# Re-ordering three stretches of a TensorE-bound attention and feed-forward kernel: other PSUM banks for block 0's last columns, batch 1's keys by values inside an output tile, batch 2's numerators later and in two pairs of banks

## Chip, cores, metric

One core of one Trainium2 chip. The metric is the device time of one execution in microseconds; medians of several executions are quoted. The span of a profile runs from its first to its last instruction and is some 1.85 us shorter than the time of the same execution.

## The reference

```python
q_p, k_p = phi(q), phi(k)              # relu, times cos and sin of the position, side by side: 128 features
kv  = einsum('bhsf,bhsd->bhfd', k_p, v)    # "keys by values", per batch and head
num = einsum('bhsf,bhfd->bhsd', q_p, kv)   # "numerators"
den = einsum('bhsf,bhf->bhs', q_p, k_p.sum(2)) + 1e-6
x   = (num / den) reshaped to 4608 tokens x 512
out = (gelu(x @ w_gate) * (x @ w_val)) @ w_out
```

8 batches of 576 tokens, 8 heads of 64; the feed-forward part has width 1536. Inputs are float32, the matmuls run in bf16.

## The kernel before

Everything is hand-scheduled: instructions run on each engine in the order in which the program names them. `ps` is the whole PSUM, eight banks of 512 float32 columns. The feed-forward part works in blocks of tokens (block 0 is batch 0's 576 tokens, then blocks of 512, the last of 448); attention of the next batch is slipped between the matmuls of a block.

```python
def kv_half(b, g, bank, eng="s"):        # keys by values of 4 heads: 20 matmuls into ps[:, bank], then a copy
    ...
def numer(b, t, bank, rows=128):         # numerators of token tile t: 8 matmuls into bank and bank + 1
    numer_mm(b, t, bank, 0, rows)
    numer_mm(b, t, bank, 1, rows)
    xb = new_xb()
    norm(xb, bank, 0, 2, rows)           # VectorE: den + eps, 1 / den, numerators * (1 / den)
    return xb
def gate(n, jt, c0, w, gb): ...          # 4 matmuls into bank gb, then ScalarE's gelu out of it
def value(n, jt, c0, w, vb): ...         # 4 matmuls into bank vb, then VectorE's multiply hT = gel * value
def o_part(n, m, bank, j0, j1): ...      # matmuls j0..j1 of the 12 of an output tile of 128 tokens
def x_by_pe(b, t, xb, bank, eng): ...    # 4 transposes on TensorE into a bank, then a copy into xT
def turn_x(b, t, xb): ...                # the same by DMA transpose from SyncE's queue
...
# block 0's last columns (A = columns 0-255, Bw = 256-575; X(t) transposes tile t, Y(t) its numerators)
gv_unit(0, 0, 256, 128, 5, 6)
X(3, 0, "s")()
gv_unit(0, 1, 256, 128, 4, 7)
Y(4, 0)()
gv_unit(0, 0, 384, 128, 5, 2)
...
# between block 0 and block 1
o_tile(0, 1, 5)
kv_half(1, 0, 6, "s")
kv_half(1, 1, 7, "v")
...
# block 1: what is put between gate and value of a unit (mid) or after it
def attn_step(b, i):
    if i == 0:
        kv_half(b, 0, 6)
        kv_half(b, 1, 7)
    else:
        turn_x(b, i - 1, numer(b, i - 1, 6))
...
mid[1][0].append(L(attn_step, 1, 5))     # batch 1's last tile
...
put(5 + s, L(attn_step, b, 0))           # batch b = 2: after unit 4, as s = -1 for block 1
for i in range(5):
    mid[n][6 + s + i].append(L(attn_step, b, i + 1))
```

Of the kernel before, what the change touches and what calls it, by code (L numbers as in the profile page):

```python
# [16 lines left out]
def kernel(  # L17
# [133 lines left out]
    def kv_half(b, g, bank, eng="s"):  # L151
        for h in range(4 * g, 4 * g + 4):
            for j in range(NJ + 1):
                nc.tensor.matmul(  # L154
                    ps[:, bank, (h % 4) * (D + 1):(h % 4 + 1) * (D + 1)],
                    lhsT=kp[:, j, h, :],
                    rhs=vx[b % 2][:, j, h, 0:D + 1],
                    start=(j == 0), stop=(j == NJ),
                )
        if eng is not None:  # L160
            kv_evac(b, g, bank, eng)

    def kv_evac(b, g, bank, eng):
        src = ps[:, bank, 0:4 * (D + 1)].rearrange("p (h e) -> p h e", e=D + 1)
        dst = kv[b % 2][:, 4 * g:4 * g + 4, 0:D + 1]
        (nc.scalar.copy if eng == "s" else nc.vector.tensor_copy)(dst, src)

    def numer_mm(b, t, bank, g, rows=128):
        for h in range(4 * g, 4 * g + 4):
            nc.tensor.matmul(  # L170
                ps[0:rows, bank + g, (h % 4) * (D + 1):(h % 4 + 1) * (D + 1)],
                lhsT=qT[b % 2][:, t, h, 0:rows],
                rhs=kv[b % 2][:, h, 0:D + 1],
                start=True, stop=True,
            )

    def norm(xb, bank, g0, g1, rows=128):

        n = g1 - g0
        nd = ps[0:rows, bank + g0:bank + g1, 0:4 * (D + 1)].rearrange("p g (h e) -> p g h e", e=D + 1)  # L180
        den = rot.tile([128, 2, 4], FP32, name="den")
        nc.vector.tensor_scalar(den[0:rows, 0:n], nd[:, :, :, D], EPS, None, op0=ALU.add)  # L182
        rec = rot.tile([128, 2, 4], FP32, name="rec")
        nc.vector.reciprocal(rec[0:rows, 0:n], den[0:rows, 0:n])
        nc.vector.tensor_tensor(  # L185
            xb[0:rows, g0:g1], nd[:, :, :, 0:D],
            rec[0:rows, 0:n, :, None].to_broadcast([rows, n, 4, D]), op=ALU.mult,
        )

    def new_xb():  # L190
        return rot.tile([128, 2, 4, D], BF16, name="xb", bufs=4)

    def numer(b, t, bank, rows=128):
# [4 lines that stand above are left out]
        norm(xb, bank, 0, 2, rows)  # L198
        return xb

    def turn_x(b, t, xb):
        p0 = b * S + t * 128
        xb2 = xb.rearrange("p g h d -> p (g h d)")
        if t < NJ:
            nc.sync.dma_start_transpose(out=xT[:, :, p0:p0 + 128], in_=xb2)
        else:
            xr = rot.tile([128, CT, 128], BF16, name="xr")
            nc.sync.dma_start_transpose(out=xr, in_=xb2)
            nc.gpsimd.tensor_copy(xT[:, :, p0:p0 + 64], xr[:, :, 0:128:2])  # L209
# [15 lines left out]
    def value(n, jt, c0, w, vb):  # L225

        p0 = starts[n] + c0
        for ct in range(CT):
            nc.tensor.matmul(  # L229
                ps[:, vb, 0:w], lhsT=wv_sb[:, ct, jt * 128:(jt + 1) * 128],  # L230
                rhs=xT[:, ct, p0:p0 + w], start=(ct == 0), stop=(ct == CT - 1),
            )
        gel = gels.pop((n, jt, c0))
        nc.vector.tensor_mul(hT[n % 2][:, jt, 64 + c0:64 + c0 + w], gel[:, 0:w], ps[:, vb, 0:w])  # L234

    def gv_unit(n, jt, c0, w, gb, vb, mid=()):
        gate(n, jt, c0, w, gb)
        for f in mid:
            f()
        value(n, jt, c0, w, vb)  # L240
# [15 lines left out]
    def o_part(n, m, bank, j0, j1):  # L256
        c0 = 128 * m - starts[n] + 64
        for jt in range(j0, j1):
            nc.tensor.matmul(  # L259
                ps[:, bank, :], lhsT=hT[n % 2][:, jt, c0:c0 + 128], rhs=wo_sb[:, jt, :],  # L260
                start=(jt == 0), stop=(jt == JT - 1),
            )
        if j1 == JT:
            o_store(m, bank)

    def o_tile(n, m, bank):

        o_part(n, m, bank, 0, JT)
# [45 lines left out]
    def load_v(b):  # L314
        load(vf, v, b)
# [20 lines left out]
    def x_by_pe(b, t, xb, bank, eng, c0=0, c1=CT):  # L336
        p0 = b * S + t * 128
        cp = nc.vector.tensor_copy if eng == "v" else nc.scalar.copy
        xb2 = xb.rearrange("p g h d -> p (g h d)")
        rows = 128 if t < NJ else 64  # L340
        view = ps[:, bank, 0:256].bitcast(BF16).rearrange("p (c t) -> p c t", c=CT)
        for ct in range(c0, c1):
            nc.tensor.transpose(  # L343
                out=view[:, ct, 0:rows], in_=xb2[0:rows, ct * 128:(ct + 1) * 128], identity=ident[0:rows, 0:rows],
            )
        cp(xT[:, c0:c1, p0:p0 + rows], view[:, c0:c1, 0:rows])  # L346

    def sq(j, which, eng, *h):
        scale(Q, j, which, eng, *h)
# [48 lines left out]
    A, Bw = (0, 256), (256, 320)  # L398
    xs = {1: x1}

    def X(t, bank, eng):
        return lambda: x_by_pe(0, t, xs[t], bank, eng)

    def Y(t, bank):
        def f():
            xs[t] = numer(0, t, bank, 128 if t < NJ else 64)
        return f
# [20 lines left out]
    value(0, 3, *A, 2)  # L428
    q_by_pe(0, 4, 3, "s")
    gv_unit(0, 0, 256, 128, 5, 6)  # L430
    X(3, 0, "s")()
    gv_unit(0, 1, 256, 128, 4, 7)
    Y(4, 0)()
    gv_unit(0, 0, 384, 128, 5, 2)
    gv_unit(0, 1, 384, 128, 4, 3)
    gate(0, 4, *A, 5)
    X(4, 0, "v")()
    gate(0, 5, *A, 4)
    gv_unit(0, 2, *Bw, 1, 6)
    gv_unit(0, 3, *Bw, 0, 7)  # L440
    value(0, 4, *A, 3)
    value(0, 5, *A, 2)
    gv_unit(0, 0, 512, 64, 4, 6)
    gv_unit(0, 1, 512, 64, 5, 7)
# [10 lines left out]
    def L(f, *a):  # L455
        return lambda: f(*a)
# [15 lines left out]
    for jt in range(4, 12):  # L472
        for i, (c0, w) in enumerate((A, Bw)):
            if (jt, i) not in ((4, 0), (5, 0)):
                gv_unit(0, jt, c0, w, i, 3 - i)
            for f in between.get((jt, i), ()):
                f()
    for j in range(NJ + 1):
# [7 lines left out]
    cast_v(1, 4, 6, "v")  # L486
    cast_v(1, 6, 8, "s")
    load_v(2)
    o_tile(0, 1, 5)
    kv_half(1, 0, 6, "s")  # L490
    kv_half(1, 1, 7, "v")
    y = [new_xb() for _ in range(4)]
    o_part(0, 2, 4, 0, 4)
    for g in (0, 1):
        numer_mm(1, 0, 0, g)
        numer_mm(1, 1, 2, g)
    norm(y[0], 0, 0, 2)
    norm(y[1], 2, 0, 2)
    o_part(0, 2, 4, 4, 8)
    for g in (0, 1):  # L500
        numer_mm(1, 2, 6, g)
    norm(y[2], 6, 0, 2)
    x_by_pe(1, 0, y[0], 0, "s")
    o_part(0, 2, 4, 8, 12)
    x_by_pe(1, 1, y[1], 1, "s")
    for g in (0, 1):
        numer_mm(1, 3, 2, g)
    norm(y[3], 2, 0, 2)
    o_part(0, 3, 5, 0, 5)
    x_by_pe(1, 2, y[2], 6, "s")  # L510
    o_part(0, 3, 5, 5, 10)
    x_by_pe(1, 3, y[3], 7, "s")
    for j in range(NJ + 1):
        sq(j, 0, "v")
    o_part(0, 3, 5, 10, 12)
    sq(0, 1, "s")

    def attn_step(b, i):

        if i == 0:  # L520
            kv_half(b, 0, 6)
            kv_half(b, 1, 7)
        else:
            turn_x(b, i - 1, numer(b, i - 1, 6))


    after = {n: {jt: [] for jt in range(JT)} for n in range(NB)}

    mid = {n: {jt: [] for jt in range(JT)} for n in range(NB)}
    mid[1][0].append(L(attn_step, 1, 5))  # L530
    for n in range(1, 7):
        b = n + 1
        a = after[n]

        def put(u, *fs):
            a[u].extend(fs)

        s = 0 if n > 1 else -1
        if n > 1:
            put(0, L(sq, 0, 0, "v"), L(sq, 1, 0, "v"), L(sq, 1, 1, "v"), L(sq, 0, 1, "s"))  # L540
            put(1, L(sq, 2, 0, "v"), L(sq, 2, 1, "s"), L(turn_q, b, 0, 3))
            put(1, L(sq, 3, 0, "v"), L(sq, 4, 0, "v"), L(sq, 4, 1, "v"), L(sq, 3, 1, "s"), L(turn_q, b, 3, 5))
        else:
            put(0, L(sq, 1, 1, "s"), L(sq, 2, 1, "v"), L(turn_q, b, 0, 3))
            put(0, L(sq, 3, 1, "v"), L(sq, 4, 1, "s"), L(turn_q, b, 3, 5))
        put(2 + s, L(sk, 0, 0, "v"), L(sk, 1, 0, "v"), L(sk, 0, 1, "s"), L(sk, 1, 1, "s"))
        put(3 + s, L(sk, 2, 0, "v"), L(sk, 3, 0, "v"), L(sk, 4, 0, "v"))
        put(3 + s, L(sk, 2, 1, "s"), L(sk, 3, 1, "s"), L(sk, 4, 1, "s"), L(cast_v, b, 0, 4))
        put(4 + s, L(cast_v, b, 4, 8, "s"))
        put(5 + s, L(attn_step, b, 0))  # L550
        if b + 1 < B:

            for f, u in zip((load_q, load_k, load_v), (3, 4, 5) if n > 1 else (1, 10, 11)):
                put(u, L(f, b + 1))
        for i in range(5):
            mid[n][6 + s + i].append(L(attn_step, b, i + 1))

    for n in range(2, NB):
        for i, m in enumerate(o_tiles_of(n - 1)):
# [47 lines left out]
```

## Time and profile before

| | before |
|---|---|
| median of the first three executions | 326.73 us (326.55 to 326.76) |
| the execution that was profiled | 327.47 us, span 325.6 us |
| TensorE busy | 318.2 us, 98% |
| VectorE, ScalarE, GpSimd busy | 52%, 46%, 7% |
| TensorE's late rows, worked out in the prediction | 1.94 us in seven places, all between 22 and 71 us |

SyncE's queue, from the timeline of the kernel before (start, time until the issue is done, queue, line, operation):

```profile
61.85 1.21 SPq L208 DMA_TRANSPOSE xr<-xb  x1
63.23 7.74 SPq L145 DMA_TRANSPOSE qT<-qp  x2
```

Batch 2's queries (`qT<-qp`) stand behind batch 1's last tile (`xr<-xb`), which stands behind the loads of batch 2. The first of the two landed at 70.73.

### The profile page before, as it was taken

To read this page: it belongs to the slowest core of one execution; us is meant where nothing else is said; L and a number is where in the kernel's file an instruction comes from. 1 tells how busy PE (TensorE), PEld (TensorE's weight loads), DVE (VectorE), ACT (ScalarE), POOL (GpSimd) and SP (SyncE) were. 2 spreads that over 40 slices of the span, in tenths; PEclk is the share of its full clock that TensorE was granted. 3 is DMA by queue.
4 is the path that set the end of the run, shared out by engine and by line. 5 is a ranking of instruction groups with operands and counts; after the bars stand their busy time and mean duration, and the time that the engine had idled before them with its cause. 6 is when DMAs were issued, how large, how long until landed. Compare 5 with 4: busy or idle time off the path is not lost.

```text
span 325.6 us, 5865 instructions
## 1 busy us (share of the span) xinstructions
PE 318.2 (98%) x2218; PEld 167.1 (51%) x2218; DVE 168.7 (52%) x380; ACT 151.3 (46%) x271; POOL 21.8 (7%) x43
## 2 busy tenths in 40 slices
PE   7999999999999999999999999999999999999994
PEld 2587866455445444554455445544554444444443
DVE  4885776768653666365736474537454222222210
ACT  5674664863483256425652475237622322323321
POOL 2651010000100010001000100010000100100000
PEclk9999999999999999999999999999999999999999
DMA  7999999999899939992899379975434111000024
GB/s 221 287 204 275 232 286 294 338 169 207 268 229 322 249 50 172 317 255 64 162 329 253 64 133 280 308 92 106 121 64 83 32 32 34 32 32 32 35 65 97
DMA packets 88300, 55.56 MB, mean 171 GB/s; under 512 B 53072, under 2 KB 83536, under 8 KB 88272
## 3 DMA queue, kind: packets, MB, share of 16 engines
q1 hardware_dynamic: 81744, 48.84, 61.7%
q0 software_dynamic: 6096, 5.90, 10.2%
q10 hardware_dynamic: 432, 0.46, 0.5%
q8 instruction: 17, 0.28, 0.4%
q14 instruction: 11, 0.09, 0.1%
HBM read 37.75 MB, written 9.44 MB: 145 GB/s over the span
## 4 chain that ended last, share of the span: by engine, by line
PE 94%; DMA 2%; DVE 1%; issue 1%; ACT 1%; ACTq 0%
PE ps L218 28%; PE ps L259 28%; PE ps L229 28%; PE ps L170 3%; PE ps L127 3%; PE ps L154 2%; DMA qT<-qp 2%; PE ps L324 1%; PE ps L277 1%; PE ps L343 1%; DVE vx L141 0%; ACT xT L346 0%; DVE qT L332 0%; DVE qp L135 0%; DVE xb L185 0%
## 5 line engine op out<-in xcount | busy, mean ns | idle before, releaser
L234 DVE TENSOR_TENSOR hT<-gel,ps 128x512 bf16<-128x512 f32 (+5 forms) x126 | 76.0, 608 | 88.8 <-PE ps L229 86.7
L218 PE MATMUL ps<-xT,wg_sb 128*128 128x512 bf16 (+5 forms) x504 | 113.4, 349 | 0.2 <-ACT xT L346 0.2
L229 PE MATMUL ps<-xT,wv_sb 128*128 128x512 bf16 (+5 forms) x504 | 113.2, 348 | 0.0
L223 ACT ACTIVATE gel<-ps 128x512 f32<-128x512 f32 (+5 forms) x126 | 67.4, 536 | 75.1 <-PE ps L218 46.6
L259 PE MATMUL ps<-wo_sb,hT 128*128 128x512 bf16 x420 | 96.5, 379 | 0.0
L218 PEld LDWEIGHTS <-wg_sb 128*128 128x128 bf16 x504 | 47.1, 98 | 45.3 <-issue 0.7
L229 PEld LDWEIGHTS <-wv_sb 128*128 128x128 bf16 x504 | 45.6, 98 | 38.9 <-issue 0.2
L259 PEld LDWEIGHTS <-hT 128*128 128x128 bf16 x420 | 40.8, 98 | 47.7
L288 ACT COPY o_sb<-ps 128x512 f32<-128x512 f32 x35 | 20.5, 586 | 75.2 <-PE ps L259 72.1
L182 DVE TENSOR_SCALAR den<-ps 128x8 f32<-128x8 f32 (+2 forms) x41 | 6.7, 165 | 44.4 <-PE ps L170 44.4
L185 DVE TENSOR_TENSOR xb<-ps,rec 128x512 bf16<-128x512 f32 (+2 forms) x41 | 27.8, 678 | 1.5
L137 ACT ACTIVATE kp<-kf,sin_c 128x512 bf16<-128x512 f32 (+1 forms) x41 | 25.4, 679 | 0.8 <-DMA kf<-in_k_dram 0.8
L170 PEld LDWEIGHTS <-qT 128*128 128x128 bf16 (+1 forms) x320 | 15.1, 98 | 9.1 <-DMA qT<-qp 0.8
L135 DVE TENSOR_SCALAR kp<-kf,cos_c 128x512 bf16<-128x512 f32 (+1 forms) x45 | 18.7, 463 | 1.4 <-DMA kf<-in_k_dram 1.4
L137 ACT ACTIVATE qp<-qf,sin_c 128x512 bf16<-128x512 f32 x28 | 19.3, 713 | 0.0
L135 DVE TENSOR_SCALAR qp<-qf,cos_c 128x512 bf16<-128x512 f32 x40 | 18.0, 492 | 0.1
L170 PE MATMUL ps<-kv,qT 128*128 128x65 bf16 (+1 forms) x320 | 16.5, 194 | 0.7 <-DMA qT<-qp 0.4
L209 POOL COPY xT<-xr 128x256 bf16<-128x256 bf16 x7 | 2.8, 401 | 198.6 <-DMA xr<-xb 198.6
L127 PE MATMUL ps<-hT 128*128 128x512 bf16 x34 | 11.0, 478 | 1.7 <-DVE par_i L104 1.7
L154 PEld LDWEIGHTS <-kp 128*128 128x128 bf16 x320 | 10.9, 97 | 2.6 <-issue 0.7
L154 PE MATMUL ps<-vx,kp 128*128 128x65 bf16 x320 | 11.1, 193 | 0.1
L141 ACT CAST vx<-vf 128x1280 bf16<-128x1280 f32 (+1 forms) x9 | 9.7, 1074 | 1.1 <-DMA vf<-in_v_dram 1.1
(54 smaller groups left out, 88.9 us busy)
## 6 DMA issues: line engine op xcount, KB each, us to landing
out_dram<-o_sb SPq DMA_DIRECT2D x38, 128.0 KB, 2.4
kf<-in_k_dram SPq DMA_DIRECT2D x7, 640.0 KB, 8.2
out_dram<-o_sb SPq DMA_DIRECT2D x16, 256.0 KB, 2.9
qf<-in_q_dram SPq DMA_DIRECT2D x6, 640.0 KB, 6.1
vf<-in_v_dram SPq DMA_DIRECT2D x6, 640.0 KB, 9.6
kf<-in_k_dram SPq DMA_DIRECT2D x7, 512.0 KB, 6.5
qf<-in_q_dram SPq DMA_DIRECT2D x6, 512.0 KB, 4.8
vf<-in_v_dram SPq DMA_DIRECT2D x6, 512.0 KB, 8.6
```

The lines of the kernel that those rows point to most:

```text
L127: nc.tensor.matmul(ps[:, bank, :], lhsT=junk[:, 0:128], rhs=junk, start=True, stop=True)
L135: nc.vector.tensor_scalar(d, s, col, 0.0, op0=ALU.mult, op1=ALU.max)
L137: nc.scalar.activation(d, s, AF.Relu, scale=col)
L154: nc.tensor.matmul(ps[:, bank, (h % 4) * (D + 1):(h % 4 + 1) * (D + 1)], lhsT=kp[:, j, h, :], rhs=vx[b % 2][:, j, h, 0:D + 1], start=(j == ...
L170: nc.tensor.matmul(ps[0:rows, bank + g, (h % 4) * (D + 1):(h % 4 + 1) * (D + 1)], lhsT=qT[b % 2][:, t, h, 0:rows], rhs=kv[b % 2][:, h, 0:D ...
L185: nc.vector.tensor_tensor(xb[0:rows, g0:g1], nd[:, :, :, 0:D], rec[0:rows, 0:n, :, None].to_broadcast([rows, n, 4, D]), op=ALU.mult,)
L218: nc.tensor.matmul(ps[:, gb, 0:w], lhsT=wg_sb[:, ct, jt * 128:(jt + 1) * 128], rhs=xT[:, ct, p0:p0 + w], start=(ct == 0), stop=(ct == CT - 1),
L223: nc.scalar.activation(gel[:, 0:w], ps[:, gb, 0:w], AF.Gelu)
L229: nc.tensor.matmul(ps[:, vb, 0:w], lhsT=wv_sb[:, ct, jt * 128:(jt + 1) * 128], rhs=xT[:, ct, p0:p0 + w], start=(ct == 0), stop=(ct == CT - 1),
L234: nc.vector.tensor_mul(hT[n % 2][:, jt, 64 + c0:64 + c0 + w], gel[:, 0:w], ps[:, vb, 0:w])
L259: nc.tensor.matmul(ps[:, bank, :], lhsT=hT[n % 2][:, jt, c0:c0 + 128], rhs=wo_sb[:, jt, :], start=(jt == 0), stop=(jt == JT - 1),)
L288: nc.scalar.copy(o_sb, ps[:, bank, :])
```

## The change

Its intent: let no engine make TensorE wait between 22 and 71 us. Three parts: other banks and another order for block 0's last columns; keys by values six matmuls earlier, with the second output tile split around them, so that more matmuls are left to cover the copies just before block 1; batch 2's first numerators behind unit 5 of block 1 and batch 1's last ones in unit 3; batch 2's five groups take banks 6/7 and 4/5 in turn.

```diff
@@ -428,17 +428,16 @@
     value(0, 3, *A, 2)
     q_by_pe(0, 4, 3, "s")
     gv_unit(0, 0, 256, 128, 5, 6)
-    X(3, 0, "s")()
-    gv_unit(0, 1, 256, 128, 4, 7)
-    Y(4, 0)()
-    gv_unit(0, 0, 384, 128, 5, 2)
-    gv_unit(0, 1, 384, 128, 4, 3)
+    gv_unit(0, 1, 256, 128, 4, 7, (X(3, 0, "s"),))
+    Y(4, 2)()
+    gv_unit(0, 0, 384, 128, 5, 1)
+    gv_unit(0, 1, 384, 128, 4, 0)
     gate(0, 4, *A, 5)
-    X(4, 0, "v")()
+    X(4, 7, "v")()
     gate(0, 5, *A, 4)
-    gv_unit(0, 2, *Bw, 1, 6)
-    gv_unit(0, 3, *Bw, 0, 7)
-    value(0, 4, *A, 3)
+    gv_unit(0, 2, *Bw, 2, 6)
+    gv_unit(0, 3, *Bw, 3, 7)
+    value(0, 4, *A, 1)
     value(0, 5, *A, 2)
     gv_unit(0, 0, 512, 64, 4, 6)
     gv_unit(0, 1, 512, 64, 5, 7)
@@ -472,7 +471,8 @@
     for jt in range(4, 12):
         for i, (c0, w) in enumerate((A, Bw)):
             if (jt, i) not in ((4, 0), (5, 0)):
-                gv_unit(0, jt, c0, w, i, 3 - i)
+                j = 0 if jt == 4 else i
+                gv_unit(0, jt, c0, w, j, 3 - j)
             for f in between.get((jt, i), ()):
                 f()
     for j in range(NJ + 1):
@@ -486,48 +486,49 @@
     cast_v(1, 4, 6, "v")
     cast_v(1, 6, 8, "s")
     load_v(2)
-    o_tile(0, 1, 5)
+    o_part(0, 1, 5, 0, 6)
     kv_half(1, 0, 6, "s")
     kv_half(1, 1, 7, "v")
+    o_part(0, 1, 5, 6, 12)
     y = [new_xb() for _ in range(4)]
-    o_part(0, 2, 4, 0, 4)
     for g in (0, 1):
         numer_mm(1, 0, 0, g)
         numer_mm(1, 1, 2, g)
     norm(y[0], 0, 0, 2)
     norm(y[1], 2, 0, 2)
-    o_part(0, 2, 4, 4, 8)
+    o_part(0, 2, 4, 0, 6)
     for g in (0, 1):
         numer_mm(1, 2, 6, g)
     norm(y[2], 6, 0, 2)
     x_by_pe(1, 0, y[0], 0, "s")
-    o_part(0, 2, 4, 8, 12)
+    o_part(0, 2, 4, 6, 10)
     x_by_pe(1, 1, y[1], 1, "s")
     for g in (0, 1):
         numer_mm(1, 3, 2, g)
     norm(y[3], 2, 0, 2)
-    o_part(0, 3, 5, 0, 5)
+    o_part(0, 2, 4, 10, 12)
+    o_part(0, 3, 5, 0, 2)
     x_by_pe(1, 2, y[2], 6, "s")
-    o_part(0, 3, 5, 5, 10)
+    o_part(0, 3, 5, 2, 7)
     x_by_pe(1, 3, y[3], 7, "s")
+    o_part(0, 3, 5, 7, 12)
     for j in range(NJ + 1):
         sq(j, 0, "v")
-    o_part(0, 3, 5, 10, 12)
     sq(0, 1, "s")
 
-    def attn_step(b, i):
+    def attn_step(b, i, bank=6):
 
         if i == 0:
             kv_half(b, 0, 6)
             kv_half(b, 1, 7)
         else:
-            turn_x(b, i - 1, numer(b, i - 1, 6))
+            turn_x(b, i - 1, numer(b, i - 1, bank))
 
 
     after = {n: {jt: [] for jt in range(JT)} for n in range(NB)}
 
     mid = {n: {jt: [] for jt in range(JT)} for n in range(NB)}
-    mid[1][0].append(L(attn_step, 1, 5))
+    mid[1][3].append(L(attn_step, 1, 5))
     for n in range(1, 7):
         b = n + 1
         a = after[n]
@@ -553,7 +554,9 @@
             for f, u in zip((load_q, load_k, load_v), (3, 4, 5) if n > 1 else (1, 10, 11)):
                 put(u, L(f, b + 1))
         for i in range(5):
-            mid[n][6 + s + i].append(L(attn_step, b, i + 1))
+
+            where = mid[n][6 + s + i] if n > 1 or i else after[n][5]
+            where.append(L(attn_step, b, i + 1, 6 if n > 1 or i % 2 == 0 else 4))
 
     for n in range(2, NB):
         for i, m in enumerate(o_tiles_of(n - 1)):
```

## The prediction

> **What bounds the kernel now.** I read the page first (busy shares, then the chain that ended last), then the list of waits, then TensorE's rows in order of time.
>
> ```profile
> PE 318.2 (98%) x2218; PEld 167.1 (51%) x2218; DVE 168.7 (52%) x380; ACT 151.3 (46%) x271; POOL 21.8 (7%) x43
> ...
> PE 94%; DMA 2%; DVE 1%; issue 1%; ACT 1%; ACTq 0%
> ```
>
> TensorE is the bound: 98% busy, 94% of the chain, nobody else above 52%. The change removes no instruction, so it can win only the time in which TensorE stands still. The list of waits shows very little of that:
>
> ```profile
> PE ps L170 <- DMA qT<-qp: 0.4, 1, 0.4
> PE ps L218 <- ACT xT L346: 0.2, 1, 0.2
> PE ps L170 <- ACT xT L346: 0.2, 1, 0.2
> ```
>
> These are three waits of 0.8 us in all (the fourth, 1.7 us, is the start of the kernel). The rows in time show more, if one subtracts starts from starts. Columns: start, length, engine, line, operation, form, count, and in brackets the idle time that the profile admits:
>
> ```profile
> 22.72 0.39 PE L229 MATMUL ps<-xT,wv_sb 128*128 128x128 bf16 x4
> 23.15 0.40 PE L343 MATMUL ps<-ident,xb 128*128 128x128 bf16 x4
> 23.38 0.39 PE L218 MATMUL ps<-xT,wg_sb 128*128 128x128 bf16 x4
> 23.61 0.39 PE L229 MATMUL ps<-xT,wv_sb 128*128 128x128 bf16 x4
> 24.22 0.41 PE L170 MATMUL ps<-kv,qT 128*64 128x65 bf16 x8 [0.23 <-ACT xT L346]
> ...
> 30.73 0.71 PE L229 MATMUL ps<-xT,wv_sb 128*128 128x320 bf16 x4
> 31.42 0.70 PE L218 MATMUL ps<-xT,wg_sb 128*128 128x320 bf16 x4
> 32.08 0.70 PE L229 MATMUL ps<-xT,wv_sb 128*128 128x320 bf16 x4
> ...
> 53.89 0.42 PE L170 MATMUL ps<-kv,qT 128*128 128x65 bf16 x8
> 54.29 0.40 PE L343 MATMUL ps<-ident,xb 128*128 128x128 bf16 x4
> ...
> 58.47 0.59 PE L259 MATMUL ps<-wo_sb,hT 128*128 128x512 bf16 x2
> 59.30 1.02 PE L218 MATMUL ps<-xT,wg_sb 128*128 128x512 bf16 x4 [0.24 <-ACT xT L346]
> ...
> 69.39 1.03 PE L218 MATMUL ps<-xT,wg_sb 128*128 128x512 bf16 x4
> 70.78 0.43 PE L170 MATMUL ps<-kv,qT 128*128 128x65 bf16 x8 [0.35 <-DMA qT<-qp]
> ```
>
> The undisturbed step from start to start is 0.216 us at 512 columns (24 of them between 45.27 and 50.45), 0.136 at 320, 0.056 at 128, and 0.032 for the 65-column ones. So the 23.15 row was due at 22.72 + 4 x 0.056 = 22.94 and is 0.21 late. Likewise: 24.22 is 0.39 late, 31.42 is 0.15, 32.08 is 0.12, 54.29 is 0.14, 59.30 is 0.40, 70.78 is 0.53. Together **1.94 us**. After 71 us I find no late row: TensorE runs without a break to the end, so all that can be won lies in these seven places, and whatever is won there reaches the end unchanged.
>
> **What the Trainium skill says.** "Perfetto Trace Analysis", section "Tensor Engine Instruction (MATMUL, LD_WEIGHTS)": the profiler computes a matmul's end from its size, it doesn't observe it. The trace agrees: a row of four 512-column matmuls is 1.03 long while the next starts after 0.865, so every wait is shown some 0.16 too short, and shorter ones not at all. "TensorE: Matmul & The Clock Gate", "Back-to-back issue gap": N/2.4 + 2.5 ns, 216 ns at 512 columns; the trace has 0.216. "PSUM — Partial Sum Buffer", "PSUM bank collisions raise a hardware error": guard a bank as a whole by semaphores, not by address. That is why a writer waits for the last reader of its bank; the 24.22 row waits for ScalarE's copy out of the bank it reuses. The same page, "Engine vs sequencer instructions": ScalarE and VectorE queues are strict FIFO, which decides the second loss below.
>
> **The change part by part.**
>
> *Block 0's last columns.* (a) The transposes of tile 3 move behind the next gate group (0.22 us of matmuls), past the end of VectorE's multiply at 23.09, which they waited for: -0.21. (b) Tile 4's numerators get banks 2 and 3 instead of the bank that tile 3's copy is leaving: their wait (0.39) goes. But the gate group behind them reads the columns that this copy writes. Transposes at 23.17, end of their output 0.40 later, ScalarE's copy at 23.63 (after a gate activation that now precedes it), 0.59 long: 24.22. The gate could start at 23.97 and starts at 24.26; before it started at 24.57. So (a) and (b) together give 0.31, not 0.60. (c) Units (4) and (5) of the 320-column half used the same banks 1 and 2 back to back; unit 4 now has 0 and 3: both late rows, 0.27, go. Here I find no new wait: the value banks 1 and 2 are read out before. Sum: **-0.58**.
>
> *Keys by values inside the second output tile.* (d) Between the last transposes of batch 1 (58.24) and block 1 stood 2 matmuls, 0.43 us, and ScalarE's copy needs 0.43 + 0.59 after the transposes start. Now 5 stand there, 1.08 us plus the transposes' own 0.22, against 1.06: the 0.40 goes. (e) Six matmuls and a numerator group, 1.56 us instead of 1.12, cover the first norm: -0.14. (f) The price: keys by values come six matmuls, 1.30 us, earlier. They started at 50.45, so they would be due at 49.15. VectorE's casts of batch 1's values run from 48.50; the first, of 0.95 us, ends at 49.45, and its vector work hangs on block 0's last multiply and so moves along with TensorE. TensorE waits **+0.35** there (a little more because ScalarE's key scaling can't move with it: those keys land at 45.03 and the work starts at 45.27). Sum: **-0.19**.
>
> *Batch 2's numerators.* (g) The first group moves behind value unit 5 (0.87 us later), and batch 1's last tile from unit 0 to unit 3, so its DMA transpose no longer stands in front of batch 2's queries in SyncE's queue: the queries' transposes were issued at 63.23 and landed at 70.73, two to three us of that behind the other transpose (landed 68.26). The wait of 0.53 goes with over a us to spare. The second pair of banks is needed because groups 1 and 2 now stand only 0.87 us apart, while one norm takes 1.13. (h) The price: batch 1's last numerators use banks 6 and 7, and batch 2's keys by values, one and a half units later, write them. Let block 1 start at T. Keys by values are due after five units of 1.73 and one numerator group of 0.26: T + 8.91. The norm stands in VectorE's queue behind unit 2's multiply (value group's start + 1.14 = T + 5.47), three key scalings (start 0.60 later), and the cast (1.19 later), and starts 0.87 after that: T + 8.13 (steps as between the rows at 65.01, 65.61, 66.80 and 67.67 of before). It ends 1.13 later, T + 9.26, so TensorE waits **+0.40**. Sum: **-0.13**.
>
> Total: -0.58 - 0.19 - 0.13 = -0.90 us, which is 1.94 less 0.29 (b), 0.35 (f) and 0.40 (h), to rounding. 326.73 - 0.90 = **325.8 us**, 0.3%.
>
> **The rivals.** *No new wait bites:* if the norm of (h) comes up earlier or the casts of (f) are in time, 1.65 are won, 325.1. For it speaks that somebody moved the group to unit 3 and not to unit 0 and presumably liked the result; against it, VectorE's rows leave no gap between 63.9 and 68.3 us. *The transfers take it back:* between 48 and 83 us loads and transposes land one after another in the order of issue, DMA mean 90% busy. They don't move when TensorE does. Batch 2's queries land at 57.34, keys at 61.30, values at 64.33, their readers start about 57.4, 62.1 and 65.8 in my working, so only the query scaling waits, on VectorE, which has two us to spare there. Block 2 needs the last transposed tile of batch 2 (landed 82.28, block 2 at 83.44); both move with TensorE. If one of them bit, half a us would go: 326.3. *The displaced work is neutral:* the three losses are larger than worked out and eat everything: 326.7. Against it: (c), (d) and (g) are waits that the new order plainly lacks.
>
> **Range and chances.** The seven gains are read to 0.02 us each; the three losses, 1.04 together, could each be off by half. Runs differ by 0.2. That gives 325.2 to 326.3. All 1.94 us are 0.6%, so faster by over 2% is ruled out if the reading is right, and a loss of 6.5 us would need a stage that breaks entirely: 0.01 each.
>
> **What would show it.** In the changed kernel's rows: units 4 and 5 of the 320 columns 0.54 apart throughout; block 1 starting without a bracket; the numerators of batch 2 without a wait on the queries' DMA; a late gate group after tile 4's numerators; batch 1's keys by values late by some 0.35 behind VectorE's cast; batch 2's late by some 0.4 behind the norm (VectorE's product of numerators and reciprocals). Wrong it would be if the last two are missing (time near 325.1), or if a late row appears after 72 us, where I expect none.

## The result

| | before | changed |
|---|---|---|
| median (6 executions each) | 326.72 us (326.55 to 326.91) | 326.46 us (326.09 to 326.54) |
| ratio | | 0.999, 95% interval 0.9978 to 1.0003 |
| span of the profile | 325.6 us | 324.7 us |
| first gate matmul to last matmul | 304.11 us | 303.15 us |
| start to first gate matmul | 16.84 us | 16.63 us |
| last matmul to the end | 4.68 us | 4.92 us |

A ratio is the mean time of one kernel's runs over that of the other's of the same rounds, so it is not quite the ratio of the medians; what follows is about differences of a few tenths of a per cent. The last three rows are taken from the starts of single matmuls in the traces and add up to the span.

The time is 0.26 us down, the prediction said 0.9, with a range that ended at 326.3. Yet the two profiles differ by 0.9. Busy time and chain of the changed kernel, from its page:

```profile
PE 317.4 (98%) x2218; PEld 167.3 (52%) x2218; DVE 168.2 (52%) x380; ACT 151.3 (47%) x271; POOL 22.0 (7%) x43
...
PE 94%; DVE 3%; issue 1%; ACT 0%; DVEq 0%
```

DMA has left the chain, VectorE has a greater share of it: the wait for the queries' DMA is gone, two waits for VectorE have come. Before asking why the time doesn't follow, the changed kernel's rows, in the same places as the prediction's (TensorE alone, start, length, line, form, count):

```profile
22.96 0.39 PE L343 MATMUL ps<-ident,xb 128*128 128x128 bf16 x4
23.18 0.39 PE L229 MATMUL ps<-xT,wv_sb 128*128 128x128 bf16 x4
23.50 0.44 PE L170 MATMUL ps<-kv,qT 128*64 128x65 bf16 x8
24.02 0.38 PE L218 MATMUL ps<-xT,wg_sb 128*128 128x128 bf16 x4
...
30.17 0.71 PE L229 MATMUL ps<-xT,wv_sb 128*128 128x320 bf16 x4
30.71 0.71 PE L218 MATMUL ps<-xT,wg_sb 128*128 128x320 bf16 x4
31.26 0.71 PE L229 MATMUL ps<-xT,wv_sb 128*128 128x320 bf16 x4
...
48.68 1.36 PE L154 MATMUL ps<-vx,kp 128*128 128x65 bf16 x40 [0.18 <-DVE vx L141]
...
57.19 1.24 PE L259 MATMUL ps<-wo_sb,hT 128*128 128x512 bf16 x5
58.27 1.03 PE L218 MATMUL ps<-xT,wg_sb 128*128 128x512 bf16 x4
...
67.55 1.37 PE L154 MATMUL ps<-vx,kp 128*128 128x65 bf16 x40 [0.23 <-DVE xb L185]
...
69.61 1.03 PE L229 MATMUL ps<-xT,wv_sb 128*128 128x512 bf16 x4
70.48 0.42 PE L170 MATMUL ps<-kv,qT 128*128 128x65 bf16 x8
```

Read the steps: 30.17, 30.71, 31.26 are 0.54 apart; block 1 starts 5 x 0.216 after the last output matmuls (57.19 to 58.27); the numerators at 70.48 start 0.87 after their predecessor. The seven late rows are gone, but for 0.09 that the numerators at 23.50 keep. And three new ones stand where the prediction put them: keys by values of batch 1 start at 48.68 and are 0.34 late (predicted 0.35), those of batch 2 at 67.55, 0.39 late (predicted 0.40), and the gate group behind tile 4's numerators starts at 24.02, 0.25 late. The rows on VectorE that they wait for, from the timeline of the changed kernel (two casts in one row; then the product that ends the norm):

```profile
47.68 1.41 DVE L141 CAST vx<-vf 128x1280 bf16<-128x1280 f32 x2
...
66.80 0.69 DVE L185 TENSOR_TENSOR xb<-ps,rec 128x512 bf16<-128x512 f32 x1
```

66.80 + 0.69 = 67.49, and TensorE goes on at 67.55. That norm's first row starts at 66.38, behind the cast at 65.51, though its numerators had started at 64.31: VectorE kept the order of its queue, as the prediction had it. The list of waits of the changed kernel says the same:

```profile
PE ps L154 <- DVE vx L141: 0.3, 2, 0.2
PE ps L154 <- DVE xb L185: 0.2, 1, 0.2
```

And SyncE's queue of the changed kernel, against the two lines above under "Time and profile before":

```profile
61.50 6.67 SPq L145 DMA_TRANSPOSE qT<-qp  x2
...
70.23 1.28 SPq L208 DMA_TRANSPOSE xr<-xb  x1
```

Batch 2's queries now stand before batch 1's last tile; the first of their two transposes landed at 68.41, some 2 us before the numerators at 70.48.

So within TensorE the prediction of this profile holds to 0.06 us (0.96 between first gate and last matmul, 0.90 predicted). What fails is the step from the two profiles to the times.

### The profile page after: what moved, and what is told of

It reads as the page before. It is cut to its first block, busy times and chain, and to the rows that moved or that the text cites. A ratio compares the mean times of both kernels' runs of the same rounds, so it can differ in the third digit from the quotient of the medians.

```text
span 324.7 us, 5863 instructions
## 1 busy us (share of the span) xinstructions
PE 317.4 (98%) x2218; PEld 167.3 (52%) x2218; DVE 168.2 (52%) x380; ACT 151.3 (47%) x271; POOL 22.0 (7%) x43
## 4 chain that ended last, share of the span: by engine, by line
PE 94%; DVE 3%; issue 1%; ACT 0%; DVEq 0%
PE ps L218 28%; PE ps L229 28%; PE ps L259 27%; PE ps L154 3%; PE ps L170 3%; PE ps L127 3%; DVE kp L135 1%; PE ps L324 1%; PE ps L277 1%; DVE vx L141 1%; PE ps L343 1%; DVE xb L185 0%; DVE rec L184 0%; ACT xT L346 0%; DVE qp L135 0%
```

## The experiments

Theories. **A**: the profiled execution of before was not a usual one; one of the seven late rows is mostly absent in a usual execution, so there was less to win. Rival **B**: it was usual, and the changed kernel loses outside TensorE's rows. For the longer end (4.92 against 4.68): **C**, it hangs on where VectorE's instruction stream ends; rival **D**, on the new order of work.

| run | time, us | ratio (95%) | first gate to last matmul | last matmul to end | to note among its late rows, 22 to 82 us |
|---|---|---|---|---|---|
| again_before | 326.63 | 0.9993 (0.9981 to 1.0006) | 303.65 | 4.68 | queries' wait 0.05, the others as before |
| again_after | 326.61 | 0.9996 (0.9984 to 1.0009) | 303.15 | 4.91 | as in the changed kernel |
| p0 | 326.22 | 0.9982 (0.9969 to 0.9994) | 303.40 | 4.68 | queries' wait 0.41 |
| p2 | 327.38 | 1.0017 (1.0003 to 1.0031) | 303.98 | 4.92 | keys by values of batch 2 0.39 |
| p1 | 326.73 | 0.9994 (0.9981 to 1.0006) | 303.38 | 4.69 | keys by values of batch 1 0.34, queries' wait none |
| fix_two | 325.90 | 0.9968 (0.9956 to 0.9981) | 302.47 | 4.91 | gate 0.25, one of 0.05 at 79 |
| fix_three | 325.66 | 0.9968 (0.9954 to 0.9981) | 302.35 | 4.93 | gate 0.10 |
| after_pad | 326.33 | 0.9980 (0.9967 to 0.9992) | 303.16 | 4.69 | as in the changed kernel |
| look_1, look_2 | 326.80, 327.26 | single runs | 303.66, 304.03 | 4.71, 4.71 | queries' wait 0.06, 0.43 |
| p2_clean | 326.66 | 0.9988 (0.9975 to 1.0002) | 303.59 | 4.69 | the before's, without the queries' wait |
| three_pad | 325.94 | 0.9963 (0.9951 to 0.9976) | 302.93 | 4.68 | three waits for DMA, 0.20, 0.10, 0.28 |

The first four ran on one chip (before there 326.91), the next four on another (327.02), the last four on a third (326.98; the first of those before-runs took 327.73, all of them between 326.63 and that). Note again_before: the same program on the same chip as its comparison, and 0.28 apart in the median. Nor does the 0.26 of the result come back: again_after is only 0.02 below again_before (one of its five executions took 327.41). Times alone settle nothing below about 0.3 us here; where less is argued, it is from single rows of the traces, which repeat to 0.01. All results were correct.

**again_before**: the kernel before, no edit.

> The kernel before, unchanged. The profile that the prediction rests on was taken of an execution of 327.47 us, 0.75 above the median of 326.72. Theory A (that execution was not a usual one): this profile spans about 324.9 us and its late matmul rows between the first gate group and block 1's keys by values sum to clearly less than the 1.94 us that I read, so there was less to win. Rival B (it was usual, and the changed kernel loses outside TensorE's rows, or in executions that were not profiled): the span is about 325.6 again with the same seven late rows. Time 326.7 either way.

Its profile spans 324.9, and six of the seven late rows come back within 0.01. The seventh doesn't. TensorE in the second profile of before; this trace has lost one of the four gate records, so its row holds three and starts one step later:

```profile
69.31 0.81 PE L218 MATMUL ps<-xT,wg_sb 128*128 128x512 bf16 x3
70.00 0.43 PE L170 MATMUL ps<-kv,qT 128*128 128x65 bf16 x8
```

69.31 + 3 x 0.216 = 69.96: the numerators are 0.05 late, not the 0.52 of the first profile. From the first gate to the last matmul it is 303.65 instead of 304.11, which is this wait; of the 0.76 between the two spans (325.63 and 324.87) the other 0.31 stands before the first gate matmul (16.84 and 16.53). Theory A holds. B falls for this part; its other half, a loss outside TensorE's rows, comes true at the kernel's end (p2, after_pad).

**again_after**: the changed kernel, no edit.

> The changed kernel, unchanged. Both theories: 326.4 to 326.5, ratio 0.999; profile with the two new waits before keys by values (0.34 and 0.39 in the first profile) and 0.25 at the gate group after tile 4's numerators. If these three differ by over 0.15 us from the first profile, the waits themselves vary between executions.

303.15 again, the three new waits 0.25, 0.34 and 0.39 again. The gain inside TensorE, against the execution of before with the short wait, is 303.65 - 303.15 = 0.50, not 0.96.

**look_1, look_2**: the kernel before, two more looks.

> The kernel before, one look. The queries' transposes landed at 70.73 in the first profile and at 69.96 in the second, and TensorE waited 0.52 and 0.05 for them. Theory A: another value between 0 and 0.6, which goes with the landing of batch 2's first query load, 0.9 us earlier in the second profile (55.61 and 54.68); all other late rows are the same within 0.01. Rival: always either 0.52 or 0.05 with nothing else changed.

> The kernel before, one more look. As for the last: the wait for the queries' transposes lies between 0 and 0.6 and follows the landing of the query load; nothing else in the late rows moves by more than 0.01.

The wait was 0.06 and 0.43. From the second look:

```profile
69.46 0.81 PE L218 MATMUL ps<-xT,wg_sb 128*128 128x512 bf16 x3
70.54 0.43 PE L170 MATMUL ps<-kv,qT 128*128 128x65 bf16 x8 [0.27 <-DMA qT<-qp]
```

In four profiles of one program it is 0.52, 0.05, 0.06 and 0.43, in executions of 327.47, 326.70, 326.80 and 327.26 us. The long waits belong to the long executions. That the usual execution has the short wait is inferred from the times: the median of the comparison, 326.72, lies by the two short ones. Only four executions were seen in a profile, and on the other chips the median of before, 326.91 to 327.02, lies between. My expectation named the first of batch 2's two query loads as what it follows; that doesn't hold (it landed at 55.61, 54.68, 53.30 and 54.00). The wait goes with the second, which landed at 57.34, 56.36, 56.34 and 57.08, and from there on everything that SyncE has issued lands in a row: the last output store before the transposes at 66.27, 65.38, 65.33 and 66.03, the queries at 70.73, 69.96, 70.04 and 70.50. Why that load lands earlier or later by 1 us stays open.

**p0**: the first two hunks of the diff alone.

> Block 0's part alone. The prediction's working: 0.58 us faster than before (326.15). Theory A with the missing size in this part: less, down to 0. Theory A with the missing size in the DMA wait for batch 2's queries: the full 0.58, unless that wait swallows it.

Between first gate and last matmul it wins only 0.25 (303.65 to 303.40) in its profile: block 0's part does give 0.6 up to the first output tile, but TensorE then stands at the numerators 0.41 until the queries land (69.69). That is only 0.27 before their landing in again_before (69.96), so a gain ahead of it can be swallowed there. In time it is 0.4 below again_before: the executions that were not profiled were up to 0.3 shorter than the profiled one.

**p1**: the third hunk down to `attn_step` (`o_part(0, 1, 5, 0, 6)`, keys by values, `o_part(0, 1, 5, 6, 12)` and the re-cut output tiles up to block 1).

> Keys by values inside the second output tile alone. The prediction's working: 0.40 and 0.14 won, 0.35 lost, 0.19 faster, 326.5. Theory A (the queries' transposes land at a time that TensorE does not set): block 1 does begin 0.19 earlier, but TensorE then waits that much longer for the queries, and the time stays within 0.1 of before.

0.27 between first gate and last matmul, with 0.34 lost as worked out; this execution had no wait for the queries: they landed at 69.54, before their numerators at 70.06. Theory A's expectation, that TensorE would wait for them for as much as it had won, did not come true here. The predicted 0.19 and theory A's "within 0.1" can't be told apart in time (ratio 0.9994).

**p2**: the rest of the diff alone, from `attn_step` on (`mid[1][3]`, `after[n][5]`, banks 4 and 6 in turn).

> Batch 2's numerators alone. The prediction's working: wait for the queries' DMA gone (-0.53), new wait of keys by values for the norm in banks 6 and 7 (+0.40): 0.13 faster. Theory A with the missing size in this part (a usual execution has hardly any wait for that DMA): 0.3 to 0.4 slower than before, 327.1, with the new wait in the rows.

The only part that loses beyond doubt: 0.75 above again_before. Its row for batch 2's keys by values is 0.39 late, and there is hardly a wait for the queries to be won. Between the two profiled executions (327.32 and 326.70, 0.62 apart) that makes 0.33 in TensorE (303.98 - 303.65); 0.24 more is at the end of the kernel: 4.92 instead of 4.68. So this part carries the longer end, too.

**after_pad**: the changed kernel and two instructions that do nothing useful.

```diff
+    for i in range(2):
+        nc.vector.memset(tiny[0:1, 2 + i:3 + i], 0.0)
     last = list(o_tiles_of(NB - 1))
```

> The changed kernel with two one-element memsets on VectorE before the last output tiles, which nothing waits for. From TensorE's last matmul to the end the changed kernel takes 4.92 us and the kernel before 4.69, because VectorE's last drain starts at 4.20 instead of 3.83. The changed kernel has two VectorE instructions fewer in its program (579 against 581). Theory C (where the end of VectorE's instruction stream falls sets that delay): with 581 again the end takes 4.69 and 0.23 comes back, span 324.3. Rival D (the delay belongs to the new order of work): 4.92 stays.

The drains of VectorE at the program's last line, from the view of one source line (count, shortest / median / longest in ns, first and last start), kernel before:

```profile
L602 DVEq DRAIN  x2: 19/174/330, 321.6 to 324.8; - x2
```

Changed kernel, and the changed kernel with the two memsets:

```profile
L605 DVEq DRAIN  x2: 119/224/330, 320.4 to 324.0; - x2
```

```profile
L607 DVEq DRAIN  x2: 19/174/330, 320.4 to 323.6; - x2
```

In the traces VectorE has 579 records before, 577 in the changed kernel and 579 with the memsets (the 581 and 579 of my expectation can't be read from them; the difference is the same). The two that are gone are no work: both kernels have 380 working instructions, and 196 against 194 semaphore instructions (EVENT_SEMAPHORE). With two fewer the last drain takes 119 ns instead of 19 and starts 3.6 us, not 3.2 us, after the one before it; with the two memsets it is as before, and the end takes 4.69. C holds, D falls: the work is in the changed kernel's order, and only the count is before's. All fourteen profiles agree: the end takes 4.91 to 4.93 in the five with 577 records and 4.68 to 4.71 in the nine with 579. "Runtime: NRT & Kernel Launch", section "Instruction fetch mechanics", says that an engine's instructions are fetched in blocks while it runs and that crossing a block is mostly hidden. A fetch that isn't hidden would fit, but no run shows one; the mechanism stays open.

**p2_clean**: p2, batch 1's last numerators in banks 4 and 5 (the edit against p2 is shown), and the two memsets of after_pad.

```diff
-    mid[1][3].append(L(attn_step, 1, 5))
+    mid[1][3].append(L(attn_step, 1, 5, 4))
```

> Batch 2's numerators alone as in p2, which lost 0.7, but batch 1's last numerators in banks 4 and 5, and the two memsets that put the end of VectorE's stream back. If p2's loss is the sum of the wait for the norm (0.39) and the later drain (0.23), both go, and the time is before's less the wait for the queries: 326.3 to 326.7. Rival (the displaced transposes and loads cost something more): 327 stays.

0.72 below p2, and as fast as again_before (326.63): 303.59 against 303.65 is the queries' wait of 0.05. It is 0.32 below the before-runs of its own rounds, but again_before, with no edit at all, was 0.28 below its own. Both the late row and the longer end are gone from the trace, so p2's loss was its two costs, as far as the times tell; and its gain, where the queries land early, is next to nothing.

**fix_two**: the changed kernel, the same bank edit, and keys by values two matmuls later.

```diff
-    o_part(0, 1, 5, 0, 6)
+    o_part(0, 1, 5, 0, 8)
...
-    o_part(0, 1, 5, 6, 12)
+    o_part(0, 1, 5, 8, 12)
```

> The changed kernel with two edits: batch 1's last numerators in banks 4 and 5, which batch 2's keys by values do not write, and batch 1's keys by values after eight matmuls of the second output tile instead of six. If the new waits are what I take them for, the two late rows (0.34 and 0.39) go and the time falls by 0.73 against the changed kernel, to about 325.8. Rival: VectorE is behind, and the wait only comes back at the next reader of its results: under 0.4 won.

0.68 in TensorE (303.15 to 302.47), both late rows gone, and 0.6 to 0.7 in time against the medians of the changed kernel (on other chips; the ratios to before are 0.9968 and 0.999). The rival falls. The end stays at 4.91.

**fix_three**: with a gate group moved ahead as well.

```diff
-    gv_unit(0, 0, 384, 128, 5, 1)
-    gv_unit(0, 1, 384, 128, 4, 0)
     gate(0, 4, *A, 5)
+    gv_unit(0, 0, 384, 128, 6, 1)
+    gv_unit(0, 1, 384, 128, 4, 0)
```

> As the last, and a gate group of 256 columns that needs no part of tile 3 stands between tile 4's numerators and the gate that reads tile 3's copy. If that late row (0.25, of which 0.10 also stood after these 64-column numerators before) is the copy: 0.15 more won, 325.6. Rival: it is the narrow weights alone, and nothing moves.

TensorE around keys by values of batch 1 and of batch 2:

```profile
45.79 2.75 PE L259 MATMUL ps<-wo_sb,hT 128*128 128x512 bf16 x12
48.38 1.37 PE L154 MATMUL ps<-vx,kp 128*128 128x65 bf16 x40
...
65.56 1.03 PE L229 MATMUL ps<-xT,wv_sb 128*128 128x512 bf16 x4
66.43 1.37 PE L154 MATMUL ps<-vx,kp 128*128 128x65 bf16 x40
```

12 x 0.216 and 4 x 0.216: nothing is late. The gate's 0.25 became 0.10, and 0.10 also stands after the 64-row numerators in every profile, the kernel before's too. A new one of 0.07 follows at 25.73, so that 0.07 of the 0.15 is left at the first output tile. The other 0.05 between 302.47 and 302.35 is fix_two's late row at 79, which this profile doesn't have. Against fix_two nothing can be told in time (both ratios are 0.9968); against both kernels this version is ahead: 325.66, ratio to before 0.9968, where the changed kernel has 0.9990 and 0.9996 (the intervals just touch or stand apart).

**three_pad**: fix_three and the two memsets.

> fix_three (three edits) with the two memsets as well. If the gains add: fix_three's 325.7 less 0.23, 325.4, end of 4.69, and about 1.3 us, 0.4%, under the kernel before.

The end is 4.68 as expected, but the time is 325.94, not 325.4; two of its five executions, 325.43 and 325.54, are there. In the profiled one (326.09) DMA was late again: 0.20 at the queries (69.89), then two value groups, 0.10 and 0.28, behind a VectorE that waited for a transpose to give up a buffer of normalized tiles:

```profile
77.70 0.69 DVE L185 TENSOR_TENSOR xb<-ps,rec 128x512 bf16<-128x512 f32 x1 [1.86 <-DMA xr<-xb]
...
79.70 0.69 DVE L185 TENSOR_TENSOR xb<-ps,rec 128x512 bf16<-128x512 f32 x1 [0.40 <-DMA xT<-xb]
```

0.57 of the gain went there. The memsets' 0.23 is seen in the trace and not resolved in time. fix_three has the same order of matmuls, and its profile has none of the three: there the queries landed at 68.36, here at 69.84. So from execution to execution the transfers of this stretch decide how much of the gain arrives.

## Why the prediction was wrong

The prediction's own steps, against an execution of before with the short wait (again_before):

| step | predicted, us | found, us | shown by |
|---|---|---|---|
| (a), (b) tile 3's transposes, tile 4's numerators, with the gate's new wait | -0.31 | -0.35: late rows of 0.20, 0.39, 0.10 became 0.10, 0.25 | rows of both kernels, again_after |
| (c) units 4 and 5 | -0.27 | -0.27 | rows, p0 |
| (d), (e) before block 1 and the first norm | -0.54 | -0.55 | rows, p1 |
| (f) keys by values, batch 1 | +0.35 | +0.34 | p1, fix_two |
| (g) wait for the queries | **-0.53** | **-0.05** | again_before, look_1, look_2 |
| (h) keys by values, batch 2 | +0.40 | +0.39 | p2, p2_clean, fix_two |
| end of the kernel | none | **+0.24** | p2, after_pad |
| sum | -0.90 | -0.25 | |

The sum is close to the measured 0.26. Part of that is luck: a sum of rows from different executions can be trusted to 0.1 only, and the second pair of medians differs by 0.02.

The step that failed is (g), "the wait of 0.53 goes": the mechanism was right, the wait goes (in the changed kernel's two profiles; 0.20 came back in three_pad's), but its size was that of one execution. It depends on when a DMA lands, and that varied by 0.8 us over four executions of the same program (69.96 to 70.73), while the six late rows that no DMA ends repeated to 0.01. The prediction said "The seven gains are read to 0.02 us each", and that was true of the reading and false of the thing read. The hint was on the table: the profiled execution took 327.47 and the median was 326.73. Had the wait that hangs on a DMA been left out for that reason, the working would have given 0.37 us and 326.4. (Only 0.46 of the difference turned out to be this wait; 0.31 stood before the first gate.)

The second miss, the 0.24 at the end, was not among the rivals at all. "The change removes no instruction" is true of the work alone: two of VectorE's semaphore instructions are gone. I had compared the order of instructions and not their number on each engine, and would not have known what two fewer mean. Of the rivals, "the transfers take it back" came nearest, but in another sense: they hadn't given it in the first place, in an execution with the short wait, and in the profiled executions of p0 and three_pad they do take part of it back.

Two readings of the prediction were also short, without moving the result. That "all that can be won lies in these seven places" passes over five more late rows after the first gate: 0.13 at 17.42 and 18.49, and 0.09 at 24.57, 26.00 and 26.22. The changed kernel has 0.13, 0.13, 0.10 and 0.09 at four of them, and the fifth is part of its 0.25. And "VectorE's rows leave no gap between 63.9 and 68.3 us" passes over an idle 0.24 before 65.01, which didn't save the norm of (h).

What the prediction got right decides what to do next. The two new waits were foreseen with their causes to 0.01, which fix_two confirms, and mending them with two small edits gave 0.68 us in TensorE, more than the change itself had won there (0.50).

## What to carry to other kernels

Before you count a wait in a profile as time to be won, ask what ends it: here the waits on an engine repeated and the wait on a DMA was a sample, so compare the profiled execution's time with the median and take a second profile. Moving work earlier on the bounding engine is worth only what the buffers and the producers' queues allow: look for the reader of the bank in the other engine's queue, and put work that is moved next to a writer of the same bank into another bank. Subtract starts from starts instead of adding up idle times. And count each engine's instructions, those on semaphores too, before and after.

## What the Trainium skill lacked or had wrong

- "Perfetto Trace Analysis", "Tensor Engine Instruction (MATMUL, LD_WEIGHTS)" says that a matmul's end is estimated, not by how much: here rows run some 0.16 us past the next possible start, so the waits of 0.12 to 0.15 us at 31.42, 32.08 and 54.29 showed as no idle time at all.
- "DMA: Bandwidth & Descriptors" gives no spread between executions: here the same query load landed between 56.34 and 57.34 in four profiles of one program, and the transposes behind it between 69.96 and 70.73.
- "Runtime: NRT & Kernel Launch", "Instruction fetch mechanics" calls the cost of crossing a block mostly hidden. No page tells of what these runs show: two VectorE instructions fewer in the trace (577 for 579, both of them semaphore instructions) made the kernel's end 0.24 us longer, 4.92 for 4.68, and two idle memsets took it back (4.69). Whether it is fetching is not shown.
- No page gives the price of a narrow matmul among full ones: the rows of 64-row transposes, and the rows behind 64-row numerators and transposes, start at least 0.09 us late in every profile. "TensorEngine Tiling (Array Packing)", "Key Properties", tells of a drain at a change of tiling mode, without a time; whether that is what happens here no run shows, and a wait this short would not be listed.
- "TensorE: Matmul & The Clock Gate", "Back-to-back issue gap", puts the spacing in a stream of weight loads and matmuls at some 131 ns for 512 columns and 81 ns for 128. Here it is 216 ns (24 bf16 matmuls between 45.27 and 50.45) and 56 ns. The section's formula for a single matmul gives 216 and 56.
